# Scaling of v in the first macro step and residuals of the second-layer weights moved to VectorE, with a new table of order numbers

## The chip, the cores and the metric

The kernel runs on one core of a Trainium2 chip. The metric is the device time of one execution in microseconds (us), lower is better. Three runs of the kernel before gave 835.08, 839.51 and 845.69 us, median 839.51 us. PE is TensorE, PEld its weight loads, DVE is VectorE, ACT is ScalarE, POOL is GpSimd, and SP is the engine that issues the DMAs.

## The reference

Three stages follow each other. A delta-rule attention keeps a 48 by 48 state per batch and head (4 batches, 8 heads, 768 steps); a SoLU layer with a layer norm follows (384 to 1024 and back), and then a gated layer (384 to 2048 and back). The inputs are float64.

```python
for t in range(S):
    y[:, :, t] = np.einsum('bhd,bhde->bhe', q[:, :, t], state)
    v_old = np.einsum('bhde,bhd->bhe', state, kt)
    state = state + bt[:, :, :, None] * np.einsum('bhd,bhe->bhde', kt, vt - v_old)
...
h = x @ w_in
sm = e / (np.sum(e, axis=-1, keepdims=True) + 1e-09)
ln = (solu - mu) / np.sqrt(var + 1e-06) * g_ln
...
h = x @ w_in2
g = h * (1.0 / (1.0 + np.exp(-1.702 * h)))
return (g @ w_out2).astype(np.float32)
```

## The kernel before

**Attention.** The 768 steps are cut into 24 blocks of 32 steps, and 4 blocks make a macro step (6 of them). `gram(n)` multiplies the keys of a block with its keys and queries (matmuls of line 568, masked on DVE in lines 583 and 589). `solve(m)` inverts the triangular systems of a macro step on DVE (`halves`, lines 649 to 656, for the first one; the long `eliminate` loop, lines 642 and 645, for the others) and sends the result through DRAM to the tile `dt` (lines 673 and 678). `recur(n)` is the serial part, block after block: v is scaled by a column of `dt` (line 736), the state times the keys is subtracted (748, 752), in the first macro step three products follow (765, 770, 757) with an ACT copy and a DVE subtraction between, the result is copied to `mv` by ACT and DVE (782, 786), the output is multiplied out (792), and the state is updated (827 or 822, then 836).

**Layers.** `layer1(n)` (the A tasks) takes 128 tokens of a block: y is scaled and split into two fp16 halves (`ysb`, lines 856 to 863), transposed by DMA, multiplied with w1 (line 874, 18 matmuls), passes the softmax and the norm on DVE, ACT and POOL (881 to 923) and is transposed by DMA to `lnt`. `layer1_out(g)` (B, line 946, 72 matmuls) takes four blocks together, and `layer2(g)` (C, lines 981 and 1008, 288 matmuls) does the last layer on 512 tokens. Each product is done as three fp16 products of a high and a low half.

**Weights.** `weights()` loads 42 tiles of float64 weights, unpacks each to fp32 on ACT and DVE (lines 479 to 491), writes the high half in fp16 (line 504) and then the residual, the low half. There are two ways for the residual. On PE two products are subtracted in PSUM (line 510, which the trace counts as two matmuls, and line 511) and ACT copies the result out (line 513). On DVE one instruction does it (line 516). The number `pe` says how many tiles, in the order of loading, go the first way: the 6 tiles of w1 and the 8 of wo1 come first, then 12 of w2 (512 columns wide) and 16 of wo2 (384 wide) mixed.

**What sets the order.** All work is given as tasks to `Plan`, with a modelled length, a due time and what it reads and writes. `emit` places one task after another on the engine that could start first, and among tasks that could start together the one with the lowest priority number, the due time plus an entry of the table `OFF` for that task group and engine. So each engine gets one fixed list of instructions, and each engine works through its list in order. Where the plan sees PE with nothing to do, from the start to 7.67 us and again from the end of the first elimination on, it writes filler matmuls of zeros into PE's list (line 351); they keep PE running and give no result. A filler in the list is carried out whether PE would have had to wait there or not.

Of the kernel before, what the change touches and what calls it, by code (L numbers as in the profile page):

```python
# [252 lines left out]
def kernel(  # L253
# [18 lines left out]
    PE, DVE, ACT, POOL, SP = nc.tensor, nc.vector, nc.scalar, nc.gpsimd, nc.sync  # L272
# [26 lines left out]
    w1 = [T("w1h", [128, K0, F1], FP16), T("w1l", [128, K0, F1], FP16)]  # L299
    wo1 = [T("wo1h", [128, K1, DM], FP16), T("wo1l", [128, K1, DM], FP16)]  # L300
# [44 lines left out]
    P = Plan()  # L345
# [7 lines left out]
    U, T0 = PRM["U"], PRM["T0"]  # L353
# [23 lines left out]
    def dve(n, f=1.0):  # L377
        return 0.145 + f * n / 960.0
# [4 lines left out]
    def pool(n):  # L383
        return 0.06 + n * 0.00207
# [296 lines left out]
    def recur(n):  # L681
# [3 lines left out]
        m, s = divmod(n, SUB)  # L685
        base = due(n)
        md = m % 2
        half_ = n >= PRM["nx"] and n < NSUB - 1
        i, ik, iv, ist, ir = n % NKT, n % 2, n % NKV, n % NST, 0
        kr, kt_, v_, st, r_, dt = ktr[i], ktb[ik], vtb[iv], stb[ist], rb[ir], dtb[md]  # L690

        def load_k():
# [3 lines left out]
            if not half_:  # L696
# [3 lines left out]
              nb=base - PRM["ld"])  # L700
# [23 lines left out]
        def load_q():  # L724
            SP.dma_start(out=st[64:64 + D, 0:2], in_=qt[n, 0])
            SP.dma_start(out=st[0:D, 2:4], in_=qt[n, 1])
        P.add("SP", 2 * ISSUE, load_q, w=[f"stq{ist}"], prio=base - 20, lat=0.6, nb=base + 10 - PRM["ld"])

        def load_p():
            for b in range(B):  # L730
                w0 = cls(b)[1]
                SP.dma_start(out=st[w0:w0 + CH, b], in_=p_dr[n % NPD][32 * b:32 * b + 32])
        P.add("SP", 4 * ISSUE, load_p, r=[f"pdr{n % NPD}"], w=[f"stp{ist}"], prio=base - 20, lat=0.35, nb=base + 10 - PRM["ld"])

        dst, dk = (r_, f"r{ir}") if n == 0 else (v_, f"vt{iv}")
        P.add("POOL", pool(384), lambda: POOL.tensor_tensor(
            out=dst, in0=v_, in1=dt[:, s, :, CH:CH + 1].to_broadcast([128, H, D]), op=ALU.mult),
            r=[f"dt{md}_{s}", f"vt{iv}"], w=[dk], prio=base - 5)

        mvs = [f"mvs{c}" for c in range(4)]  # L740
        b1, b2, b3, b4 = Bank(SIDE), Bank(SIDE), Bank(SIDE), [Bank(SIDE), Bank(SIDE)]

        def hd(b):
            return bank(b)[:, 0:H * D].rearrange("p (h c) -> p h c", h=H)

        def ks(h, b):
            r0 = cls(b)[0]
            PE.matmul(hd(b1)[32 * b:32 * b + 32, h, :], lhsT=kr[r0:r0 + D, b % 2, h, :],
# [342 lines left out]
```

## Time and profile before

| what | value |
|---|---|
| median of three runs | 839.51 us |
| the profiled execution: its own time | 836.79 us |
| the profiled execution: its span | 835.1 us |
| PE busy | 777.1 us, 93% of the span |
| DVE busy | 589.5 us, 71% |
| ACT busy | 373.1 us, 45% |
| POOL busy | 247.2 us, 30% |
| mean granted clock of PE | 0.969 |

The span is the time from the first to the last instruction of the profile; the execution's own time is 1.69 us longer. A granted clock of 1.00 is PE at 2.4 GHz, and the lower level is 1.2 GHz, so a mean of 0.85 in a stretch means that PE had the lower level in 30% of it. Starts and ends are in us from the start of the span. Matmuls are pipelined, so the length of a run of equal matmuls is read from start to start.

### The profile page before, as it was taken

What the parts mean: (1) busy time and instruction counts of PE and PEld (TensorE: products, weight loads), DVE (VectorE), ACT (ScalarE), POOL (GpSimd) and SP (SyncE); (2) the same over time, 40 slices, a digit from 0 to 9 for tenths busy, and PEclk for the clock granted to TensorE, in tenths of its full rate; (3) what the DMA queues carried; (4) which work ended last, traced back from release to release, by engine and by line L of the source; (5) the groups of instructions that cost most, each with busy time, mean ns of one, the idle gap of its engine ahead of it and who ended that gap; (6) DMA issues with size and microseconds to landing.
All of it is one profiled execution on the core that took longest, in us unless ns stands there. A gap on an engine that the chain in (4) does not pass through costs nothing.

```text
span 835.1 us, 25208 instructions
## 1 busy us (share of the span) xinstructions
PE 777.1 (93%) x10642; PEld 389.7 (47%) x10642; DVE 589.5 (71%) x1456; ACT 373.1 (45%) x661; POOL 247.2 (30%) x240
## 2 busy tenths in 40 slices
PE   6568978999989999998999999999999999999997
PEld 4135554444555444544544444444444444444443
DVE  2896777999999999999999899964566445212111
ACT  0467564544326524544633545525554355422332
POOL 3020011110413354325531434504442222420322
PEclk7778898999999999999999999999999999999999
DMA  6898597976646466677736654365433252100101
GB/s 168 235 278 232 148 220 137 235 196 168 125 94 139 86 149 171 147 177 159 168 79 187 142 119 104 84 152 144 103 79 94 80 115 44 26 1 0 39 1 38
DMA packets 177314, 105.76 MB, mean 127 GB/s; under 512 B 128273, under 2 KB 161169, under 8 KB 177201
## 3 DMA queue, kind: packets, MB, share of 16 engines
q1 hardware_dynamic: 177200, 104.15, 52.7%
q8 instruction: 83, 1.36, 0.7%
q14 instruction: 31, 0.25, 0.1%
HBM read 66.16 MB, written 20.64 MB: 104 GB/s over the span
## 4 chain that ended last, share of the span: by engine, by line
PE 53%; DVE 27%; issue 9%; DMA 4%; ACT 3%; POOL 2%; POOLq 0%; SPq 0%; ACTq 0%; DVEq 0%
PE psum L1008 13%; PE psum L981 13%; PE psum L946 9%; PE psum L874 6%; DVE mv L836 4%; DVE trip L645 4%; DVE trt L642 4%; PE psum L568 3%; DVE th L989 2%; PE psum L351 2%; DVE mv L786 2%; DVE col L881 2%; PE psum L510 2%; ACT mv L782 2%; DVE eb L893 2%
## 5 line engine op out<-in xcount | busy, mean ns | idle before, releaser
L995 POOL TENSOR_TENSOR gl<-th,gh 128x512 f16<-128x512 f32 x90 | 107.3, 1192 | 236.0 <-ACT gh L992 167.8
L989 DVE SCALAR_TENSOR_TENSOR th<-th,psum 128x512 f32<-128x512 f32 x96 | 65.5, 683 | 89.0 <-ACT th L986 88.4
L1008 PE MATMUL psum<-gl,wo2h 128*128 128x512 f16 x288 | 109.1, 379 | 1.0 <-POOL gl L995 1.0
L1008 PE MATMUL psum<-gh,wo2h 128*128 128x512 f16 x288 | 109.5, 380 | 0.2 <-ACT gh L992 0.2
L981 PE MATMUL psum<-x2th,w2h 128*128 128x512 f16 x288 | 109.5, 380 | 0.1
L981 PE MATMUL psum<-x2th,w2l 128*128 128x512 f16 x288 | 109.1, 379 | 0.0
L981 PE MATMUL psum<-x2tl,w2h 128*128 128x512 f16 x288 | 109.1, 379 | 0.0
L1008 PE MATMUL psum<-gh,wo2l 128*128 128x512 f16 x288 | 109.1, 379 | 0.0
L986 ACT ACTIVATE th<-psum 128x512 f32<-128x512 f32 x96 | 56.9, 593 | 98.4 <-PE psum L981 93.6
L874 PE MATMUL psum<-w1h,xt 128*128 128x512 f16 x288 | 94.2, 382 | 1.5 <-DVE mv L836 0.8
L992 ACT ACTIVATE gh<-th 128x512 f16<-128x512 f32 x96 | 60.2, 627 | 68.9 <-DVE th L989 64.6
L1008 PEld LDWEIGHTS <-wo2h 128*128 128x128 f16 x576 | 56.2, 98 | 67.9 <-issue 2.1
L981 PEld LDWEIGHTS <-w2h 128*128 128x128 f16 x576 | 53.5, 98 | 62.0 <-issue 0.3
L642 DVE TENSOR_TENSOR trt<-trip 128x30 f32<-128x30 f32 (+9 forms) x150 | 71.3, 476 | 2.7
L645 DVE TENSOR_TENSOR trip<-trip,trt 128x30 f32<-128x30 f32 (+9 forms) x150 | 69.6, 464 | 2.4
L923 POOL TENSOR_TENSOR lnr<-eb,lnr 128x1024 f16<-128x1024 f32 x24 | 52.2, 2173 | 52.0 <-ACT lnr L921 52.0
L874 PEld LDWEIGHTS <-xt 128*128 128x128 f16 x432 | 40.0, 98 | 49.9 <-issue 2.5
L890 ACT ACTIVATE eb<-psum,col 128x512 f32<-128x512 f32 x48 | 36.9, 773 | 52.4 <-DVE col L886 52.1
L946 PE MATMUL psum<-lnth,wo1h 128*128 128x512 f16 x144 | 54.6, 379 | 0.4 <-DVE th L989 0.4
L874 PE MATMUL psum<-w1l,xt 128*128 128x512 f16 x144 | 54.8, 381 | 0.0
L946 PE MATMUL psum<-lnth,wo1l 128*128 128x512 f16 x144 | 54.6, 379 | 0.0
L946 PE MATMUL psum<-lntl,wo1h 128*128 128x512 f16 x144 | 54.6, 379 | 0.0
(210 smaller groups left out, 1246.6 us busy)
## 6 DMA issues: line engine op xcount, KB each, us to landing
kq<-kq SPq DMA_DIRECT2D x44, 192.0 KB, 4.4
stg<-w_in SPq DMA_DIRECT2D x11, 512.0 KB, 5.6
vt<-vt SPq DMA_DIRECT2D x24, 192.0 KB, 2.7
st<-qt SPq DMA_DIRECT2D x48, 96.0 KB, 2.9
kt<-kdr SPq DMA_DIRECT2D x48, 96.0 KB, 2.3
stg<-udr SPq DMA_DIRECT2D x48, 96.0 KB, 2.3
out<-ob SPq DMA_DIRECT2D x18, 256.0 KB, 2.7
ktr<-kd SPq DMA_DIRECT2D x46, 96.0 KB, 2.9
```

Source lines behind the costliest of these rows:

```text
L642: DVE.tensor_tensor(out=tv, in0=tri[:, lo:hi, j:j + 1].to_broadcast([128, nr, j]), in1=tri[:, j:j + 1, 0:j].to_broadcast([128, nr, j]), op ...
L645: DVE.tensor_tensor(out=tri[:, lo:hi, 0:j], in0=tri[:, lo:hi, 0:j], in1=tv, op=ALU.add)
L874: PE.matmul(bank(bh[j]), lhsT=x[:, k], rhs=w_[:, k, 512 * j:512 * j + 512], start=(k == 0 and i == 0), stop=(k == K0 - 1 and i == 2))
L890: P.add("ACT", act(512) + 0.34, lambda j=j, ev=ev: ACT.activation(out=ev, in_=bank(bh[j]), func=ACTF.Exp, bias=cl(3), scale=cl(0), accum_o ...
L923: P.add("POOL", pool(F1), lambda: POOL.tensor_tensor(out=lnr[1], in0=e_, in1=lnr[0], op=ALU.subtract), r=["lnrh"] + [f"eb{ie}_{j}" for j i ...
L946: PE.matmul(bank(ba)[:, 0:w_], lhsT=wo1[a][:, k, oc], rhs=lnt[b][:, k, tk], start=(k == 0 and i == 0), stop=(k == K1 - 1 and i == 2))
L981: PE.matmul(bank(bh)[:, 0:w_], lhsT=w2[a][:, k, fc], rhs=x2t[b][:, k, tk], start=(k == 0 and j == 0), stop=(k == K0 - 1 and j == 2))
L986: P.add("ACT", act(w_), lambda: ACT.activation(out=th, in_=bank(bh)[:, 0:w_], func=ACTF.Tanh, scale=0.851 / (X2S * W2S)), r=[bh], w=[f"th{ ...
L989: P.add("DVE", dve(w_), lambda: DVE.scalar_tensor_tensor(out=th, in0=th, scalar=1.0, in1=bank(bh)[:, 0:w_], op0=ALU.add, op1=ALU.mult), r= ...
L992: P.add("ACT", act(w_), lambda: ACT.activation(out=gh, in_=th, func=ACTF.Copy), r=[f"th{i}"], w=[f"gh{i}"], prio=base)
L995: P.add("POOL", pool(w_), lambda: POOL.tensor_tensor(out=gl, in0=th, in1=gh, op=ALU.subtract), r=[f"th{i}", f"gh{i}"], w=[f"gl{i}"], prio= ...
L1008: PE.matmul(bank(acc[o])[:, 0:w_], lhsT=wo2[a][:, f, oc], rhs=gb[i][b][:, 0:w_], start=(f == 0 and j == 0), stop=(f == K2 - 1 and j == 2))
```

## The change

Three things are changed. The scaling of v for blocks 0 to 3 (`m == 0`) goes from POOL to DVE. `pe` goes from 38.322 to 14, so that only the tiles of w1 and wo1 get their residual on PE, and the 24 tiles of w2 and wo2 that did so before get it on DVE, where the last four already were. And all numbers of `OFF` are new, so every engine has another order.

```diff
-OFF = {'gram0|SP': 42.93, 'gram0|PE': 207.21, 'gram0|DVE': 422.4,
+OFF = {'gram0|SP': -73.65, 'gram0|PE': 157.32, 'gram0|DVE': -184.67,
...
-PRM = dict(bl=161.965, vm=-0.684, vo=-1.262, pe=38.322, near=22.976,
+PRM = dict(bl=161.965, vm=-0.684, vo=-1.262, pe=14, near=22.976,
...
         dst, dk = (r_, f"r{ir}") if n == 0 else (v_, f"vt{iv}")
-        P.add("POOL", pool(384), lambda: POOL.tensor_tensor(
+        eng, cost, E_ = ("DVE", dve(384), DVE) if m == 0 else ("POOL", pool(384), POOL)
+        P.add(eng, cost, lambda: E_.tensor_tensor(
             out=dst, in0=v_, in1=dt[:, s, :, CH:CH + 1].to_broadcast([128, H, D]), op=ALU.mult),
-            r=[f"dt{md}_{s}", f"vt{iv}"], w=[dk], prio=base - 5)
+            r=[f"dt{md}_{s}", f"vt{iv}"], w=[dk], prio=base - 5, port=True)
```

The diff puts one more line into the kernel, so line 736 and all behind it have a number higher by one in the changed kernel.

**PE, from the last matmul of block 3's first layer to the first of B0.** Before, this piece of the list holds the last w1 product of block 3 (`xt_95`), four gram quads (line 568), fillers (`zeros_157`) and four residual tiles (`eye`, `neg`). Before:

```order
L874 MATMUL psum_69<-w1h,xt_95 128x512
L568 MATMUL psum_70<-kq_112 32x64 x32
L351 MATMUL psum_63<-zeros_157 128x512
L510 MATMUL psum_66<-fst_89,eye 128x512
L511 MATMUL psum_66<-w2h,neg 128x512
L510 MATMUL psum_70<-fst_89,eye 128x384
L510 MATMUL psum_66<-ob_109,eye 128x384
L510 MATMUL psum_68<-ob_110,eye 128x512
L946 LDWEIGHTS wo1h
```

Now:

```order
L875 MATMUL psum_70<-w1h,xt_95 128x512
L351 MATMUL psum_63<-zeros_157 128x512
L568 MATMUL psum_67<-kq_112 32x64 x32
L568 MATMUL psum_69<-kq_111 32x64 x32
L568 MATMUL psum_70<-kq_112 32x64 x32
L947 LDWEIGHTS wo1h
```

Rows that repeat are left out. The residual tiles are gone from the piece, the four gram quads stay, and the fillers go from 55 to 126 (15, 10, 47, 11 and 43 between the quads). In the whole list the fillers go from 128 to 245 and the residual tiles from 38 to 14.

**DVE, the norm of block 3** (`col_138` holds its column of numbers; lines 901 and 908 are the end of the first and the start of the second part of the norm, between which ACT squares the row). Before:

```order
L901 TENSOR_TENSOR col_138<-col_138 128x1
L645 TENSOR_TENSOR trip<-trip,trt 128x28x3
L583 TENSOR_TENSOR gsb_122<-psum_70,mask 128x256
L642 TENSOR_TENSOR trt<-trip 128x108
L583 TENSOR_TENSOR psb_124<-psum_70,mask 128x256
L645 TENSOR_TENSOR trip<-trip,trt 128x27x4
L481 TENSOR_SCALAR stg_86<-stg_86 128x384
L642 TENSOR_TENSOR trt<-trip 128x130
L908 SCALAR_TENSOR_TENSOR col_138<-col_138 128x1
```

Now, the first rows behind the end of the first part, two of the three residuals that stand there, and the last rows:

```order
L902 TENSOR_TENSOR col_138<-col_138 128x1
L645 TENSOR_TENSOR trip<-trip,trt 128x28x3
L481 TENSOR_SCALAR wo2l<-wo2l 128x384
L642 TENSOR_TENSOR trt<-trip 128x108
L483 SCALAR_TENSOR_TENSOR fst_87<-fst_87,wo2l 128x384
L516 SCALAR_TENSOR_TENSOR wo2l<-fst_87,wo2h 128x384
L516 SCALAR_TENSOR_TENSOR w2l<-fst_89,w2h 128x512
L645 TENSOR_TENSOR trip<-trip,trt 128x22x9
L642 TENSOR_TENSOR trt<-trip 128x210
L909 SCALAR_TENSOR_TENSOR col_138<-col_138 128x1
```

Between the two parts stood 7 instructions and stand 27 now. From the `ysb` instruction of block 3 (line 863) to the last column instruction of its norm (line 916) there were 65 and are 91.

**DVE, the first scalings of v.** The scaling (line 737) of blocks 0 and 1 now stands among the unpacking of weights:

```order
L491 SCALAR_TENSOR_TENSOR fst_88<-stg_86,fst_88 128x512
L481 TENSOR_SCALAR wo2l<-wo2l 128x384
L483 SCALAR_TENSOR_TENSOR w2l<-w2l,wo2l 128x384
L737 TENSOR_TENSOR rb_132<-vt_120,dt_130 128x384
L491 SCALAR_TENSOR_TENSOR w2l<-wo2l,w2l 128x384
L737 TENSOR_TENSOR vt_121<-vt_121,dt_130 128x384
L516 SCALAR_TENSOR_TENSOR w2l<-fst_88,w2h 128x512
```

Before, these were the first work that POOL had after its constants, with nothing of its list in front; now 20 DVE rows stand between the end of the solve's output and the first of them.

## Rows read from the trace of the kernel before

**Rows 1.** The page: span, and busy time (share of the span) of each engine.
```profile
span 835.1 us, 25208 instructions
PE 777.1 (93%) x10642; PEld 389.7 (47%) x10642; DVE 589.5 (71%) x1456; ACT 373.1 (45%) x661; POOL 247.2 (30%) x240
```
**Rows 2.** Busy time by stretch: stretch, its length, engines (instructions), clock, DMA share.
```profile
core 0: us, PE busy (x) PEld busy (x) DVE busy (x) ACT busy (x) POOL busy (x), PEclk, DMA share, GB/s
0.00:46.00 46.00, 24.06 (x552) 12.22 (x552) 25.86 (x78) 13.08 (x22) 7.57 (x30) 0.74 0.76 219
46.00:138.50 92.50, 77.75 (x1756) 46.19 (x1756) 68.86 (x165) 56.17 (x112) 12.11 (x8) 0.85 0.83 196
138.50:175.94 37.44, 36.19 (x623) 19.52 (x624) 34.26 (x106) 18.58 (x32) 5.52 (x4) 1.00 1.00 207
175.94:700.00 524.06, 509.94 (x7117) 253.53 (x7116) 434.42 (x1062) 239.15 (x420) 184.97 (x167) 1.00 0.55 128
700.00:835.10 135.10, 129.17 (x597) 58.22 (x595) 26.10 (x48) 46.11 (x76) 37.05 (x31) 1.00 0.09 21
```
**Rows 3.** Waits of PE from 46 to 176 us: line, waited for, us, times, longest.
```profile
PE psum L748 <- issue: 4.8, 2, 2.5
PE psum L792 <- DVE mv L786: 2.3, 1, 2.3
PE psum L827 <- issue: 1.9, 1, 1.9
PE psum L765 <- issue: 1.4, 1, 1.4
PE psum L568 <- issue: 0.8, 1, 0.8
```
**Rows 4.** Timeline of PE at three places of the recurrence: start, us, what.
```profile
138.50 0.89 PE L792 MATMUL psum<-mv,st 112*32 112x48 f32 x64 [2.29 <-DVE mv L786]
...
150.69 0.39 PE L874 MATMUL psum<-w1h,xt 128*128 128x512 f16 x1 [0.43 <-DMA xt<-ysb]
...
175.94 0.38 PE L946 MATMUL psum<-lnth,wo1h 128*128 128x512 f16 x1
```
**Rows 5.** Timeline of PE: gram quad, fillers, residual tiles; read start to start.
```profile
157.97 1.10 PE L568 MATMUL psum<-kq 48*32 48x64 f32 x64
159.00 2.98 PE L351 MATMUL psum<-zeros 128*128 128x512 f16 x13
161.82 1.02 PE L510 MATMUL psum<-fst,eye 128*128 128x512 f32 x2
...
162.89 1.67 PE L351 MATMUL psum<-zeros 128*128 128x512 f16 x7
...
172.61 0.81 PE L510 MATMUL psum<-fst,eye 128*128 128x384 f32 x2
...
173.42 0.81 PE L510 MATMUL psum<-ob,eye 128*128 128x384 f32 x2
```
**Rows 6.** Timelines of POOL and PE at the first scaling of v.
```profile
58.22 3.35 POOL L736 TENSOR_TENSOR rb<-vt,dt 128x384 f32<-128x384 f32 x1 [49.19 <-DMA dt<-ddr]
...
61.62 0.57 PE L765 MATMUL psum<-rb,dt 32*32 32x48 f32 x34 [2.18 <-POOL rb L736]
```
**Rows 7.** Instructions of the v scaling: count, shortest/median/longest ns, first and last start.
```profile
L736 POOL TENSOR_TENSOR vt<-vt,dt x23: 837/843/1286, 61.5 to 661.8; 128x384 f32<-128x384 f32 x23
```
**Rows 8.** Instructions of the residual on DVE, columns as in the group before.
```profile
L516 DVE SCALAR_TENSOR_TENSOR wo2l<-ob,wo2h x2: 549/550/550, 195.6 to 203.1; 128x384 f16<-128x384 f32 x2
```
**Rows 9.** Timeline of DVE in the norm of block 3, and POOL beside it.
```profile
142.61 0.62 DVE L863 SCALAR_TENSOR_TENSOR ysb<-psum,col,ysb 128x384 f16<-128x384 f32 x1
...
164.01 0.16 DVE L916 TENSOR_TENSOR col<-col 128x1 f32<-128x1 f32 x1
...
169.67 2.29 DVE L642 TENSOR_TENSOR trt<-trip 128x198 f32<-128x198 f32 x1
...
169.45 2.29 POOL L923 TENSOR_TENSOR lnr<-eb,lnr 128x1024 f16<-128x1024 f32 x1 [5.67 <-ACT lnr L921]
```

More of the change, by code (lines that the diff above doesn't have):

```diff
@@ new lines @@
+PRM = dict(bl=161.965, vm=-0.684, vo=-1.262, pe=14, near=22.976, al=0.0, af=0.658, xp=25.764, lp=1.945, go1=24.87, so1=49.904, ew=48, nx=6.743, kp=13.711, need=100.793, fg=0.161, f1=7.669, f3=1796.849, sp=0.084, gp=0.667, gq=99, cold=25.151, cf=-1.14, nb4=9.499, v1b=1.424, cut=0.473, el=22.0, la=0.602, d0=-55.31, d1=-18.518, d2=6.18, d3=1.2, a0=14.438, wo1s=1.606, nk=15.164, nb2=1.269, nb3=7.307, early=21.447, v1=-9.577, wa=0.829, U=36.161, T0=31.882, g0=0.697, a=-0.318, b=0.937, ao=18.661, go=231.282, gs=-2.989, so=-0.04, ss=0.661, w1=-840.745, wo1=-7.28, w2o=-52.255, w2s=8.446, wo2o=41.493, wo2s=4.056, nb=1.319, bs=0.333, cs=4.152, su=8.832, ld=47.69)
```

3 lines of the change are left out of this document (1 added, 2 removed).

## The prediction

> **What bounds the kernel now.** I read the page first: PE is busy for 93% of the span, the next engine for 71% [rows 1]. So a change can pay in two ways only: less work on PE, or less waiting of PE. Next I read the busy times by stretch [rows 2]. From 175.94 us, where the first product of B0 starts [rows 4], to the end PE is busy 509.94 + 129.17 = 639.1 of 659.2 us, at the full clock; that part is PE's own work. Before it PE is idle for 21.9 + 14.8 + 1.3 = 38.0 us, and from 46 to 138.5 us it runs at a mean clock of 0.85, which is the lower level in 30% of the time. The change acts almost only in this first part. Third, the waits of PE there [rows 3]: the four kinds called "issue", in which PE waits for nothing that the profile shows, sum to 8.9 us, and the longest wait for an engine within the recurrence is 2.3 us, for DVE. Fourth, the timeline [rows 4]: the fourth output product of the recurrence starts at 138.50, block 3's first layer at 150.69, B0 at 175.94. I use the first and the last of these as cuts, so the span has three pieces: up to 138.50, the 37.44 us to B0, and the 659.2 us after.
>
> **The prices.** From [rows 5], start to start at the full clock: 13 fillers from 159.00 to 161.82 are 0.217 each; a residual tile of 512 columns from 161.82 to 162.89 is 1.07; one of 384 columns from 172.61 to 173.42 is 0.81; a gram quad from 157.97 to 159.00 is 1.03. Two matmuls of a first layer stand for 0.43, as two fillers do, since they have the same shape.
>
> **The residuals leave PE, and fillers come in.** The 24 tiles are 12 of 512 and 12 of 384 columns: 12 x 1.07 + 12 x 0.81 = 22.6 us less on PE. The list has 117 fillers more: 117 x 0.217 = 25.4 us. So PE as a whole gets 2.8 us more to do, and the question is only where. I count the lists by the three pieces.
> - Up to 138.50, from the first product of the recurrence at 61.62 [rows 6]: 14 tiles fewer (7 of each width, -13.2), 47 fillers more (+10.2), one gram quad fewer (-1.0), three first-layer matmuls more (+0.6): -3.3 us at the full clock. At the clock of this stretch that is 3.3 / 0.85 = 4.0. Its bounds are 0 (PE would have waited there for the recurrence anyway) and 6.6 (all of it at the lower level). I take 4.0, since the mean clock is the nearest row.
> - From there to B0: 7 tiles fewer (3 of 512, 4 of 384, -6.4), 92 fillers more (+20.0), a quad more (+1.0), three first-layer matmuls fewer (-0.6): +13.9 us. PE is idle for 37.44 - 36.19 = 1.25 us of this stretch [rows 2] and at the full clock, so work that is put into its list can hide 1.25 us at most: +12.7 to +13.9. I take 12.7. This is the firmest term of the sum, because fillers are in PE's list whatever happens elsewhere, and the B0 products stand behind them.
> - After B0: two tiles of 512 fewer (-2.1), one quad fewer (-1.0), two fillers fewer (-0.4): -3.6 us, PE's own work, so it counts in full. Bounds: the 20.1 us in which PE is idle after B0 can shrink or grow with the new order; I take half of it each way as its bound, 10 us, and zero as the value.
>
> ACT loses 24 copies out of PSUM. It is idle for 36 of 92.5 us in the second stretch [rows 2], and the long waits of the recurrence are not for it [rows 3], so a freer ACT is worth nothing here; it could only bring copies to `mv` forward, and then the state update on DVE is what comes late next.
>
> **The residuals on DVE.** One takes 0.55 us at 384 columns [rows 8], of 512 columns none is in the trace: between the 0.55 and, in proportion to the columns, 0.73; I take 0.7. 24 are about 15 us on DVE, and 20 of all residuals stand ahead of B0's first result now. DVE is busy for 34.26 of the 37.44 us ahead of B0 [rows 2], so here it could become late. Its list from block 3's `ysb` to the end of that block's norm has 91 instructions in place of 65; the 65 took 142.61 to 164.17, 21.6 us or 0.33 each [rows 9], so 26 more are 8.6 us. The way from `ysb` to B0 took 175.94 - 142.61 = 33.3 and would take 41.9; counted from the cut, 4.1 us earlier, that is 46.0 us. PE's list needs 37.44 + 12.7 = 50.1 us for the same way. So the residuals on DVE are hidden behind the fillers, with 4.1 us to spare. Where they aren't, every us beyond these 4.1 counts.
>
> The Trainium skill, page "Perfetto Trace Analysis", section "Optimizing Scalar/DVE Operations", speaks against this part: where the Vector engine is saturated, it would give work away to Scalar or even GPSIMD, and this change does the reverse. By it the 8.6 us would count in full instead of nothing; by the rows of the lists they lie behind fillers, and I keep the sum and give the rule a rival.
>
> **The scaling of v.** The first one took 3.35 us on POOL [rows 6], four times the 0.84 us of the others [rows 7], and PE's first product waited for it. On DVE it is one operation on 384 columns, like the residual: 0.55. The gain is 2.8 us if DVE takes it up at once. The 20 rows ahead of it are mostly unpacking work that DVE had at that time before as well; if six of them are still ahead when `dt` lands, at 0.55 each, the gain turns into 6 x 0.55 - 2.8 = 0.5 of loss. These are the bounds; I take 2.8, since DVE has the same work there as before. The other three scalings were done long before they were needed: nothing, and 1.7 us more on DVE behind PE's work.
>
> **The sum.** -2.8 (v) - 4.0 (recurrence) + 12.7 (fillers ahead of B0) - 3.6 (after B0) = +2.3 us. The profiled execution took 836.79 us, so 839.1; the median of the runs was 839.51, 2.7 us above that execution and well inside the spread of the runs. I predict 839 us.
>
> **The rivals.**
> - *The recurrence becomes quick.* For it: its stretch from 61.62 to 138.50 holds 8.9 us of "issue" waits [rows 3] and half-clock running worth 0.15 x 65 = 9.8 us (65 being 84% of the 76.9 us, the busy share of the second stretch in [rows 2]). With residuals gone from between its products, both could vanish: 839 - 8.9 - 9.8 = 820 us. Against it: fillers stand at the same places, nothing in the change takes away an "issue" wait, and PE's list does not get shorter. 15%.
> - *DVE becomes late* (the skill's rule). Place: the first macro step. 12 residuals (6.5 us at about 0.55) and four scalings (2.2 us) stand in DVE's list ahead of block 3's `ysb`, and the products of the recurrence wait for DVE at each block. If they all lie on the path, the gains of 2.8 and 4.0 are lost and 8.7 us come on top; and if POOL and DVE hold each other up as at 169.45, where an elimination step took the 2.29 us of the POOL operation beside it [rows 9], twice in the norm of block 3, that is 4.6 and uses up the 4.1 that were spare. Then 839 + 6.8 + 8.7 = 855, and 859 with two more such holds. It decides from the point at which DVE's queue adds more than 6.8 us to the recurrence. 12%.
> - *The change does nothing*, since fillers took the place of the tiles and the spare time is used elsewhere: 836 to 838 us. It can't be told from my forecast by the time, only by the place of B0, and is part of it.
>
> The forecast has 73%; its own range is 828 to 850 (the distances of the bounds from the values taken, 10 us for the waits after B0 among them, as the root of the sum of their squares: 10.3 down, 11.3 up). With part of the two rivals, the range for 8 times in 10 is 821 to 855. About 2% is what a measurement of this kernel can tell from no change, here 16.8 us: faster means under 822.7, slower over 856.3. The first rival ends at the edge of that, the second mostly inside it: 0.14 faster, 0.76 same, 0.10 slower.
>
> **What would show it.** In the profile after, the first recurrence product should start about 2.8 us after `dt` lands sooner than before, the fourth output product near 132, and B0 near 181 with PE at the full clock and without idle time for about 50 us before it; from B0 to the last instruction there should be about 655 us. The forecast is wrong if B0 starts before 170 or after 190, or if PE waits for DVE for more than 5 us between the two cuts.

## The result, and the profile after

The changed kernel takes 845.01 us (median of 20 runs, 840.08 to 850.09) against 839.52 us for the kernel before (20 runs, 832.69 to 850.84): a ratio of 1.0074, with a 95% interval of 1.0051 to 1.0098. It is 0.7% slower. No change was forecast, at 839.0 us. The time lies inside the range, but the whole interval of the ratio lies above 1, and two of the four terms of the sum missed by 5 and 9 us, in opposite directions.

The page of the changed kernel, span and engines, answers to [rows 1]:

```profile
span 838.4 us, 25263 instructions
PE 775.9 (93%) x10687; PEld 386.5 (46%) x10687; DVE 584.9 (70%) x1484; ACT 363.0 (43%) x637; POOL 244.6 (29%) x236
```

PE is busy for 1.2 us less than before here, and for 5.4 us more in the second profiles below (773.7 and 779.1 us); the prediction had counted 2.8 us more. DVE has 28 instructions more and is yet busy for 4.6 us less; the last section comes back to that. The same kernel by stretch, columns as in [rows 2], cut at its own B0:

```profile
0.00:46.00 46.00, 25.19 (x555) 12.68 (x556) 27.95 (x82) 13.43 (x22) 7.56 (x30) 0.73 0.79 220
46.00:138.50 92.50, 80.84 (x2106) 47.11 (x2105) 79.35 (x203) 48.86 (x95) 6.05 (x4) 0.95 0.86 207
138.50:172.37 33.87, 33.32 (x389) 16.42 (x388) 30.03 (x92) 13.65 (x22) 8.08 (x4) 1.00 1.05 216
172.37:700.00 527.63, 504.55 (x6980) 250.47 (x6981) 419.03 (x1056) 239.24 (x421) 185.88 (x167) 1.00 0.55 126
700.00:838.40 138.40, 132.03 (x670) 59.84 (x668) 28.58 (x56) 47.80 (x78) 37.07 (x31) 0.99 0.08 21
```

Behind B0, PE is busy for 504.55 + 132.03 = 636.6 of 666.0 us: 29.4 us idle, where it was 20.0 before. Its timeline at the places of [rows 4] and [rows 6] (first product of the recurrence, fourth output product, block 3's first layer, the fillers ahead of B0, B0):

```profile
56.54 0.36 PE L766 MATMUL psum<-rb,dt 32*32 32x48 f32 x14 [0.53 <-DVE rb L737]
...
121.11 0.27 PE L793 MATMUL psum<-mv,st 112*32 112x48 f32 x2
...
135.84 0.39 PE L875 MATMUL psum<-w1h,xt 128*128 128x512 f16 x1 [1.17 <-DMA xt<-ysb]
...
163.08 9.45 PE L351 MATMUL psum<-zeros 128*128 128x512 f16 x43
172.37 0.38 PE L947 MATMUL psum<-lnth,wo1h 128*128 128x512 f16 x1
```

One profile is one execution, and this one took 840.1 us, the shortest of its 20 runs. So both kernels were profiled a second time.

**Two more profiles.** No edit.

> The kernel before, profiled a second time: how far the pieces of one profile can be trusted. If they repeat, first product at 61 to 62 us, B0 at 175 to 177, tail 658 to 661 with 19 to 21 us of PE idle. If one execution is only a draw, the tail is 663 us or more, and the 659.2 that the prediction's sum used was a short one.

> The changed kernel, profiled a second time, since the profile shown (840.1 us) is the shortest of its runs (median 845.0). If pieces repeat, first product at 56 to 58 us, B0 at 172 to 173, tail 665 to 667 us. If the first profile was a lucky draw in the first macro step: first product at 59 to 61, B0 at 175 to 177; if in the tail: a stretch of lower clock there, tail 669 us or more.

Measured: 837.35 and 845.11 us. The two last stretches (B0 to 700 us, 700 us to the end) of the kernel before, second profile:

```profile
173.12:700.00 526.88, 509.46 (x7115) 253.08 (x7114) 437.49 (x1057) 238.94 (x419) 184.82 (x167) 1.00 0.54 127
700.00:835.60 135.60, 129.74 (x600) 58.46 (x598) 26.59 (x51) 46.35 (x76) 37.06 (x31) 1.00 0.09 21
```

and of the changed kernel, second profile:

```profile
176.50:700.00 523.50, 499.32 (x6890) 248.05 (x6889) 417.29 (x1041) 235.87 (x414) 185.79 (x166) 1.00 0.54 126
700.00:843.40 143.40, 136.98 (x752) 62.24 (x750) 32.51 (x69) 50.96 (x86) 37.61 (x32) 0.99 0.08 21
```

By the same cuts, from the two profiles of each (us):

| piece | before | changed | difference of means | forecast |
|---|---|---|---|---|
| to the first product | 61.6, 62.4 | 56.5, 58.1 | -4.7 | -2.8 |
| to the fourth output product | 76.9, 73.9 | 64.6, 67.8 | -9.2 | -4.0 |
| to B0 | 37.4, 36.9 | 51.3, 50.6 | +13.8 | +12.7 |
| B0 to the end | 659.2, 662.5 | 666.0, 666.9 | +5.6 | -3.6 |
| PE busy behind B0 | 639.1, 639.2 | 636.6, 636.3 | -2.7 | -3.6 |
| PE idle behind B0 | 20.0, 23.3 | 29.4, 30.6 | +8.3 | 0 (10 either way) |

The first three pieces sum to -0.1 us: B0 starts at 175.9 and 173.1 us before, at 172.4 and 176.5 after. The whole difference, 5.5 us, stands behind B0, and is the difference of the medians. Both expectations of a lucky draw came true in part: the 659.2 us on which the sum rested was a short one, and the changed kernel's first macro step was 4 us quicker in the first profile than in the second.

The waits of PE from B0 to the end show where the 8.3 us lie (line, waited for, us, times, longest). Before, first profile:

```profile
PE psum L792 <- ACT mv L782: 3.5, 6, 1.1
PE psum L748 <- DVE mv L836: 3.3, 11, 0.6
PE psum L792 <- DVE mv L786: 2.0, 6, 0.7
PE psum L757 <- DVE rb L752: 1.9, 3, 1.4
PE psum L1008 <- POOL gl L995: 1.0, 2, 0.7
PE psum L874 <- DVE mv L836: 0.8, 2, 0.6
```

After, first profile (lines one higher):

```profile
PE psum L793 <- ACT mv L783: 3.5, 10, 0.8
PE psum L793 <- DVE mv L787: 3.3, 8, 1.1
PE psum L758 <- DVE rb L753: 3.0, 6, 0.8
PE psum L1009 <- POOL gl L996: 2.6, 5, 0.7
PE psum L749 <- DVE mv L837: 2.5, 8, 0.6
PE psum L875 <- DMA xt<-ysb: 2.0, 2, 1.3
PE psum L793 <- DVE fst L802: 1.7, 1, 1.7
```

No wait is longer than 1.7 us, and no engine stands out: the loss is many waits under 1 us, at products of the recurrence (L793, L758), at the second layer's products for `gl`, at first layers for their transposed input. And DVE does not have more to do there: from B0 to 700 us it is busy for 434.4 and 437.5 us before, for 419.0 and 417.3 after. PE and DVE both idle more. That reads as an order of work that fits less well; the experiments ask whether it is that.

### The profile page after: what moved, and what is told of

It reads as the page before. It is cut to its first block, busy times and chain, and to the rows that moved or that the text cites. A ratio compares the mean times of both kernels' runs of the same rounds, so it can differ in the third digit from the quotient of the medians.

```text
span 838.4 us, 25263 instructions
## 1 busy us (share of the span) xinstructions
PE 775.9 (93%) x10687; PEld 386.5 (46%) x10687; DVE 584.9 (70%) x1484; ACT 363.0 (43%) x637; POOL 244.6 (29%) x236
## 5 line engine op out<-in xcount | busy, mean ns | idle before, releaser
L982 PEld LDWEIGHTS <-w2h 128*128 128x128 f16 x576 | 54.3, 98 | 64.6 <-issue 1.3
L924 POOL TENSOR_TENSOR lnr<-eb,lnr 128x1024 f16<-128x1024 f32 x24 | 54.7, 2281 | 53.7 <-ACT lnr L922 53.6
L645 DVE TENSOR_TENSOR trip<-trip,trt 128x30 f32<-128x30 f32 (+9 forms) x150 | 67.3, 449 | 2.3
L912 POOL TENSOR_TENSOR col<-col,half 128x1 f32<-128x1 f32 x24 | 14.5, 604 | 180.7 <-DVE col L910 143.5
L351 PE MATMUL psum<-zeros 128*128 128x512 f16 x245 | 60.0, 393 | 7.4 <-DVE zeros L350 6.8
L642 DVE TENSOR_TENSOR trt<-trip 128x30 f32<-128x30 f32 (+9 forms) x150 | 63.6, 424 | 2.2
L891 ACT ACTIVATE eb<-psum,col 128x512 f32<-128x512 f32 x48 | 36.9, 773 | 58.3 <-DVE col L887 58.2
L837 DVE SCALAR_TENSOR_TENSOR mv<-psum,mv 48x384 f32<-48x384 f32 x92 | 51.1, 555 | 5.8 <-PE psum L823 3.6
```

The lines of the kernel that those rows point to most:

```text
L351: P.fill.append((gate, until, lambda: PE.matmul(psum[0], lhsT=z, rhs=z.unsqueeze(1).to_broadcast([128, 4, 128]), start=True, stop=True)))
L642: DVE.tensor_tensor(out=tv, in0=tri[:, lo:hi, j:j + 1].to_broadcast([128, nr, j]), in1=tri[:, j:j + 1, 0:j].to_broadcast([128, nr, j]), op ...
L645: DVE.tensor_tensor(out=tri[:, lo:hi, 0:j], in0=tri[:, lo:hi, 0:j], in1=tv, op=ALU.add)
L924: P.add("POOL", pool(F1), lambda: POOL.tensor_tensor(out=lnr[1], in0=e_, in1=lnr[0], op=ALU.subtract), r=["lnrh"] + [f"eb{ie}_{j}" for j i ...
L982: PE.matmul(bank(bh)[:, 0:w_], lhsT=w2[a][:, k, fc], rhs=x2t[b][:, k, tk], start=(k == 0 and j == 0), stop=(k == K0 - 1 and j == 2))
```

## The experiments

**How an order was held.** The planner makes another order whenever a task changes its engine, so a part of the change cannot be undone in the source without all tasks moving. So most kernels here take their order, filler counts and PSUM banks from a table; with a kernel's own table this gives that kernel's own instruction lists.

```
-    def emit(self, sem=SEM, log=None):
-        ...                                  # choose the next task by priority and modelled time
+    def emit(self, log=None):
+        for item in ORDER.split():           # task, fillers ahead of it, banks
+            at, n, banks = re.match(r"(\d+)(?:f(\d+))?((?:b\d)*)$", item).groups()
+            ...
+            for _ in range(int(n or 0)):
+                self.fill[0][2]()
+            t.fn()
```

**1. The changed kernel, behind B0 in the old order.**

```
 ORDER = changed kernel's up to the first product of B0
-        + changed kernel's from there
+        + what is left, in the order of the kernel before
```

> The changed code in the changed order up to the first product of B0; from there on the tasks stand in the order that the kernel before has. Theory A (the loss lies in the order after B0, which puts less other work between dependent products): B0 starts near 172.4 us as in the changed kernel, the rest takes 657 to 660 us instead of 666.0, so the span is about 831 and the ratio to the kernel before 0.992 to 0.996. Rival B (the first macro step leaves its work behind: what DVE or the queues have not done at B0 is paid for later): the rest stays at 665 to 667 us, ratio 1.006 to 1.008. In between, both have a part.

Measured: ratio 1.0109 (1.0063 to 1.0155); B0 at 177.4, the rest 669.5 us, PE idle for 29.8. Theory A fails here: the old order is no better behind the new first macro step. The clock shows one reason. This kernel from 184 us on, columns as in [rows 2]:

```profile
184.00:196.00 12.00, 10.88 (x110) 5.20 (x109) 9.61 (x22) 4.64 (x9) 0.00 (x0) 1.00 0.44 144
196.00:202.00 6.00, 1.55 (x7) 0.55 (x6) 5.75 (x18) 2.64 (x5) 0.00 (x0) 0.90 0.28 89
202.00:208.00 6.00, 6.00 (x75) 2.73 (x73) 5.90 (x17) 2.02 (x4) 0.00 (x0) 0.53 0.38 87
```

PE waited for 4.45 of 6 us, and then ran the next 6 us at nearly the lower level. With a second such place at 244 to 256 us this cost some 5 us ((1 - 0.90) x 6 + (1 - 0.53) x 6, and 1.7 by the same sum at the second). From the second block of 512 tokens on (first product of B1) the old order takes 539.0 us here, and 535.1 and 538.4 in the two profiles of its own kernel (541.5 with v on DVE, experiment 5); so most of what it lost, it lost in the first block, at the seam, where one order goes over into the other (130.6 us to B1 instead of 124.1 in both profiles before).

**2. The kernel before, behind B0 in the new order.**

```
 ORDER = kernel before's up to the first product of B0
-        + kernel before's from there
+        + what is left, in the order of the changed kernel
```

> The code before in the order before up to the first product of B0; from there on the order of the changed kernel. Theory A: B0 near 175.9 us, the rest 666 to 669 us (two residual tiles of PE remain, 2.1 us), ratio 1.008 to 1.012. Rival B: the rest stays at 659 to 661, ratio 0.999 to 1.002.

Measured: 1.0114 (1.0068 to 1.0160); B0 at 177.9, the rest 672.0 us, PE idle for 29.6 us. As theory A had it, with a longer rest. Here too the clock fell twice (220 to 232 and 244 to 256 us, some 3.5 us); without that and the 2.1 us of two tiles it is 666.4, the time of the changed kernel. From B1 on the new order takes 542.4 us here, 541.9 and 542.2 in its own kernel. The idle time of the whole rest tells little, since it was 29.8 us in experiment 1 too, in the old order. From B1 on, where no seam disturbs, PE is idle for 21.8 us here, for 21.8 and 22.3 in the changed kernel, and in the old order for 14.9 and 18.4 (the two profiles before), 18.7 (1) and 21.1 (5). The old order takes 535.1 to 541.5 us there (these four executions, mean 538.5), the new one 541.9 to 542.4 (three). The experiments still to come narrow this: 3, 6, 7 and 8, in the old order, take 539.6, 541.3, 540.9 and 541.3 us from B1 on, and 4, in the new one, 541.5, so that the means are 2.4 us apart (539.6 and 542.0) and the ranges touch.

What the order does by itself shows best at the output products of the recurrence. Behind B0 they wait 5.3 to 6.5 us in all in eight executions of the old order (both profiles before, 1, 3, 5, 6, 7, 8), whatever the code, and 8.5 to 9.4 us in four of the new one (both profiles of the changed kernel, 4, and this one with the old code). Step by step the waits are those of the order: at steps 9, 16 and 17 they are 1.44, 1.12 and 1.03 us here, 1.09, 1.65 and 1.03 in the first profile of the changed kernel, and 0.23, 0 and 0 in the first before.

**3. The new code in the old order, nothing in place of the tiles.**

```
 ORDER = kernel before's, task by task
-PE, ACT   residual of w2/wo2 tile, copy     x24
+DVE       residual of w2/wo2 tile           x24
-POOL      scaling of v, n = 0 to 3
+DVE       scaling of v, n = 0 to 3
```

> The changed code (24 residuals and the four scalings of v on DVE) with every task at the place that it has in the kernel before, and with that kernel's 128 fillers, so that no filler takes the place of the tiles. Theory A (DVE has room for the residuals; only fillers and the new order ate the gain): PE has 20 us less to do ahead of B0, of which about half shows, since chains through DVE end there: B0 near 165, the rest 656 us, ratio 0.985 to 0.990. Rival C (DVE becomes late): 15 us more on DVE lie on the way, B0 at 180 to 188, ratio 1.004 to 1.013.

Measured: 1.0066 (1.0037 to 1.0096); B0 at 174.7, the rest 668.2. Neither place of B0 was right: PE had 22.6 us less to do, and B0 came when it always comes. Its stretch from 46 to 138.5 us shows what went against it:

```profile
46.00:138.50 92.50, 71.74 (x1710) 44.96 (x1710) 76.66 (x185) 49.73 (x98) 5.71 (x4) 0.75 0.83 204
```

The mean clock is 0.75, where it was 0.85 and 0.92 in the two profiles before and 0.95 and 0.91 in those of the changed kernel. Experiment 8, the same kernel with 98 fillers in place of the tiles, has 0.91. So the residual tiles had kept PE busy between the small products of the recurrence, and without them or fillers the lower clock takes back what their absence gives: the recurrence to its fourth output product takes 80.1 us, not less than the 76.9 and 73.9 before.

**4. The changed kernel with 54 fillers fewer ahead of B0.**

```
 PE, ahead of the gram quad at 162 us:
-    11 fillers
 PE, ahead of the first product of B0:
-    43 fillers
```

> The changed kernel without the last two groups of fillers ahead of B0 (43 and 11, 54 x 0.217 = 11.7 us of PE). Theory of the prediction (the way through DVE from block 3's output to B0 has 4.1 us to spare behind the fillers): B0 4.1 us earlier, near 168.3, PE idle for about 7.6 us where the fillers stood, ratio 1.002 to 1.004. Rival D (only the fillers hold B0): B0 near 160.7, ratio 0.993 to 0.995. Rival E (the granted clock falls to its lower level in the gap): a mean clock under 1.0 in the 20 us around B0 and B0 not earlier than 172 us, ratio 1.006 or more. The part after B0 is the same in all three, 664 to 667 us.

Measured: 1.0073 (1.0040 to 1.0106), the changed kernel's time. From the fourth output product to B0 it takes 49.4 us, 1.6 us less than the mean of the two executions with all fillers, though 11.7 us of fillers are gone. PE's timeline ahead of B0:

```profile
156.73 6.21 PE L255 MATMUL psum<-zeros 128*128 128x512 f16 x28
162.87 1.99 PE L472 MATMUL psum<-kq 48*32 48x64 f32 x128
172.69 0.59 PE L851 MATMUL psum<-lnth,wo1h 128*128 128x512 f16 x1 [7.83 <-DMA lnth<-lnr]
```

Where the fillers stood, PE waits 7.83 us for the transposes of block 3's norm. So B0 is held by the way through that norm, which DVE has in its list between other work, and the fillers cover this way; they don't make it longer. The end of the first part of the norm and the start of the second stand in DVE's timeline, first profile before and then first profile of the changed kernel, at:

```profile
160.85 0.16 DVE L901 TENSOR_TENSOR col<-col 128x1 f32<-128x1 f32 x1
...
162.75 0.22 DVE L908 SCALAR_TENSOR_TENSOR col<-col 128x1 f32<-128x1 f32 x1
```

```profile
147.94 0.16 DVE L902 TENSOR_TENSOR col<-col 128x1 f32<-128x1 f32 x1
...
160.82 0.22 DVE L909 SCALAR_TENSOR_TENSOR col<-col 128x1 f32<-128x1 f32 x1
```

Between the two parts lie 1.9 us before and 12.9 us in the changed kernel (1.9 and 12.6 in the second profiles, 12.4 here). In experiments 3, 6 and 8, which have the residuals on DVE but the old order, it is 2.3 us. So the place that the norm got in DVE's new list, and not the residuals by themselves, uses up what the quicker recurrence had gained. The forecast had 4.1 us to spare behind the fillers; it is 1.6. Rival D falls. Rival E's numbers came, though not as its reason had it: B0 is late for the transposes, and the clock falls in the gap and is down behind it (mean 0.50 from 172 to 178 us, 0.74 to 184), which is about 4 us of the 670.2 us that the rest takes, and the time is no shorter. So these 54 fillers neither cost nor gain: what their absence gives at B0 the clock takes back.

**5. The scaling of v alone, old order.**

```
-        P.add("POOL", pool(384), lambda: POOL.tensor_tensor(
+        eng, cost, E_ = ("DVE", dve(384), DVE) if m == 0 else ("POOL", pool(384), POOL)
+        P.add(eng, cost, lambda: E_.tensor_tensor(
```

> The kernel before in its own order, with the four scalings of v on DVE in place of POOL and nothing else. Theory of the prediction: the first product comes 2.3 to 2.8 us earlier (near 59) and the whole kernel with it, ratio 0.996 to 0.998, the tail after B0 at 659 to 662 us. Rival (something else holds the recurrence or B0, the DMA of the weights for one): the first product earlier, but B0 within 1 us of 175.9 and ratio 0.999 to 1.001. That would also mean that the 2.8 us of the sum were never to be had.

Measured: 0.9992 (0.9965 to 1.0019). The first product starts at 58.6 us, 3.4 earlier than the mean before, so the local gain is there; B0 starts at 175.5. The rival holds: the gain ends in the recurrence, whose fourth output product is at 138.5, as in [rows 4] (136.3 in the second profile before).

**6. The residuals alone, old order, fillers at the tiles' places.**

```
-PE, ACT   residual of w2/wo2 tile, copy     x24
+DVE       residual of w2/wo2 tile           x24
+PE        5 (512 columns) or 4 (384) fillers, at the 22 places ahead of B0
```

> The kernel before in its own order, v on POOL, with the 24 residuals on DVE; at the places of the 22 tiles that stood ahead of B0 PE gets fillers of the same length (5 for 512 columns, 4 for 384; 98 in all), so that it has the same work and the same claim to its clock as before. Theory A (what the change loses is lost by PE's order, not by DVE): B0 at 175 to 178 us, mean clock of 46 to 138.5 us at 0.83 to 0.87, tail 656 to 661 us with 19 to 22 us of PE idle, ratio 0.997 to 1.002. Rival C (DVE, busy over 90% of the time from 46 to 500 us, gets late by the residuals): B0 at 180 or later or the tail at 664 to 670 with 26 us of idle or more, ratio 1.006 to 1.015. Where the clock lies under 0.83, the fillers did not replace the tiles and the run says nothing of DVE.

Measured: 1.0030 (1.0006 to 1.0054); clock 0.89 from 46 to 138.5 us, so PE kept it; B0 at 174.8, the rest 667.3, PE idle for 29.2. Now the order is the same, DVE has the 24 residuals more (0.54 to 0.69 us each, one of 1.17), and it is slower, by less than rival C had it. One place can be read. DVE, which has no idle time here, and then PE:

```profile
195.10 0.68 DVE L420 SCALAR_TENSOR_TENSOR w2l<-fst,w2h 128x512 f16<-128x512 f32 x1
...
200.17 1.90 DVE L567 TENSOR_TENSOR dsb<-trip,nrm 128x1024 f32<-128x1024 f32 x1
202.00 0.67 DVE L893 SCALAR_TENSOR_TENSOR th<-th,psum 128x512 f32<-128x512 f32 x1
```

```profile
202.72 0.38 PE L885 MATMUL psum<-x2th,w2h 128*128 128x512 f16 x1 [3.49 <-DVE th L893]
```

PE's next group waits 3.49 us for DVE's `th`, which stands in DVE's list behind the residual and the 1.90 us of the solve. Before, with B0 1.2 us later, DVE did this `th` at 200.71, 1.29 us sooner.

**7. The same, the two late residuals left on PE.**

```
-        if nst[0] <= PRM["pe"]:
+        if nst[0] <= PRM["pe"] or (name, c0) == ("w2", 1536) and k > 0:
```

> The kernel with fillers for the 22 tiles (the old order, v on POOL, ratio 1.003), but the two residuals that stand behind B0 stay on PE as in the kernel before; 22 are on DVE. Theory H (behind B0 DVE has no idle time and PE waits for it product by product, so that the late residuals count there): the waits of 1.2 and 3.5 us at 195 and 203 us and the lower clock behind them go, tail 661 to 664 us in place of 667.3, ratio 0.997 to 1.001. Rival I (the 22 early residuals cost the 0.3%, through DVE's backlog at B0): tail 665 to 668, ratio 1.002 to 1.005.

Measured: 1.0038 (1.0008 to 1.0069), the rest 665.3 us. The 3.49 us wait falls to 1.06, and PE's idle time in the first block from 7.7 to 5.1 us, as theory H had it, but the time does not follow: rival I by the ratio. How the 22 early residuals cost time behind B0, which starts no later than before (175.6 us), these profiles don't show.

**8. Both parts of the code, old order, fillers at the tiles' places.**

```
 the table of 6, and
-POOL      scaling of v, n = 0 to 3
+DVE       scaling of v, n = 0 to 3
```

> Both parts of the change (24 residuals and the four scalings of v on DVE), every task at its place in the kernel before, and 98 fillers at the places of the 22 tiles that stood ahead of B0, so that PE's claim to its clock stays. Against the changed kernel (ratio 1.0074) only the order differs. Theory J (the new order costs as much as the code): 0.3% for the residuals less 0.1% for v, ratio 1.001 to 1.004, tail 663 to 667 us. Rival K (the code costs all of it, and the parts add up badly when DVE gets both): ratio 1.006 to 1.009, tail 667 us or more. A ratio of 1.005 tells neither.

Measured: 1.0036 (1.0009 to 1.0062), the rest 666.7 us. Theory J. The code change, with its fillers, costs about 0.36% in the old order; the changed kernel costs 0.74%, which leaves 0.38% to the new order. From the half widths of the two intervals that difference is uncertain by 0.36% (the root of 0.24 squared plus 0.27 squared), so that the order has a part is just shown, the halves are not. The changed kernel differs from this one by its 19 further fillers too (245 to 226). And the profiles don't show where its part lies: the rest takes 666.7 us here, at the border between the two theories, and 666.0 and 666.9 in the changed kernel, and B0 is at 172.6 against 172.4 and 176.5.

**9. More cover in the changed kernel.** Between the small products of a step (`dr`, whose result ACT and DVE copy, and `ym`, which needs the copies) the lists have groups of three large matmuls, 0.65 us each. Behind B0 the old order has three or more such groups between them at every step; the new one has two at steps 5, 8 and 22, two with a gram quad at 7, 12 and 15, and one with a gram quad at 6 and 14.

```
 PE, step 9:
-  dr9  C1 C0 C0        ym9  C1 C1
+  dr9  C1 C0 C0 C1 C1  ym9
 PE, step 12:
-  C1 C1     dr12  gram21 C1 C1  ym12  C1 C1
+  C1 C1 gram21 C1 dr12 C1 C1 C1 ym12
 ... (11 output products by 1 to 3 groups, 4 products ahead of them by 1)
```

> The changed kernel, with the order of PE alone altered behind B0: at 11 steps of the recurrence the output product stands one to three groups of three large matmuls (0.65 us each) further behind the product whose copies it waits for, at 4 steps the product ahead of it one group. Nothing else moves. Theory F (the loss after B0 is a lack of cover: where two groups stand between dependent products in place of three, PE waits): of the 12 to 13 us that these products wait after B0 in the two profiles of the changed kernel, 8.9 go (6.7 at output products, 2.2 at the others); PE idle after B0 from 30 to about 21, tail 657 to 659 us, ratio 0.996 to 0.999. Rival G (the recurrence or DVE is the bound; a product that stands later only passes its wait on to the next one): idle stays at 27 to 31, tail 664 to 668, ratio 1.005 to 1.009.

Measured: 1.0139 (1.0095 to 1.0183); the rest 673.1 us, PE idle for 35.0. The waits that were to go did go: the output products wait 2.1 us behind B0 instead of 8.7 and 9.4, the products ahead of them 0.5 instead of 3.0 and 3.7. And others came. This kernel's longest from B0 on (L913 and L886 are the second layer's products, L779 the first layer's):

```profile
PE psum L913 <- POOL gl L900: 5.2, 8, 1.1
PE psum L886 <- DVE fst L706: 4.1, 2, 2.2
PE psum L779 <- DVE eb L798: 3.4, 1, 3.4
PE psum L779 <- DMA xt<-ysb: 2.1, 3, 1.4
```

The groups that now stand ahead of `ym` wait themselves, because DVE does its list in its own order. At one of them DVE's timeline reads:

```profile
339.60 0.55 DVE L691 COPY mv<-psum 32x384 f32<-32x384 f32 x1
341.19 0.56 DVE L691 COPY mv<-psum 32x384 f32<-32x384 f32 x1 [1.04 <-ACT mv L687]
341.78 0.56 DVE L706 SCALAR_TENSOR_TENSOR fst<-psum,dt 128x384 f32<-128x384 f32 x1
```

while PE's next group, `psum<-x2th,w2h`, waits 2.23 us to 342.40 for a bank. Rival G, and worse than it had it. Some 5 us of the rest are the clock's: behind PE's wait of 3.4 us for `eb` at 243 us it is 0.50 from 244 to 250 us. Altering the order of one engine alone did not mend this kernel. Nor is the count of groups the whole of it: at the eight steps named above, where the new order has fewer than three whole groups, the output products wait 4.0 us in all in the new order and 3.3 in the old (means of the four and the eight executions of experiment 2), at the steps with three or more 5.0 and 2.8. So most of the longer waits stand where the cover was not short by this count.

**10. The same in the kernel before, with v on DVE.**

```
 PE, step 14:
-  dr14  C2 C2 C2        ym14  C2 C2
+  dr14  C2 C2 C2 C2 C2  ym14
 ... (10 output products by 1 or 2 groups, 2 products ahead of them by 1)
```

> The kernel before in its own order, v on DVE, residuals on PE as before, with the same treatment: 10 output products one or two groups later, two products ahead of them one group. Theory F: 5.9 us of waits go (5.4 and 0.5), PE idle after B0 from 20 to 26 (three executions of this order) to 15 to 20, tail 655 to 660 us, ratio 0.990 to 0.994; it would beat both kernels. Rival G: tail as in those executions, 659 to 666 us, ratio 0.997 to 1.001.

Measured: 0.9968 (0.9936 to 1.0000), the rest 662.6 us, PE idle for 23.0. The ratio lies just under rival G's range and above theory F's, and the idle time is the mean of the three earlier executions of this order (23.1). The output products wait 0.6 us instead of 5.5 and 6.5, and it comes back elsewhere (`gl` 3.4 us instead of 1.0). It has the lowest ratio of the study, below the changed kernel's 1.0074; against the kernel before its interval just reaches no change, and from v alone (0.9992, experiment 5) it can't be told apart.

**11. Less cover in the kernel before.**

```
 PE, step 14:
-  dr14  C2 C2 C2  ym14  C2
+  dr14  C2 C2  ym14  C2 C2
 ... (the output products of steps 6 to 23, one group earlier)
```

> The kernel before, untouched but for the output products of steps 6 to 23 of the recurrence, which stand one group of three large matmuls earlier: the cover is taken away that the changed order lacks. Theory F: ten of these steps wait already and would wait 0.65 us longer, 6.5 us; the other eight between nothing and 5.2 us; PE idle after B0 26 to 34 us, tail 667 to 674, ratio 1.007 to 1.014. Rival G: no change beyond 2 us, ratio 0.998 to 1.002.

Measured: 1.0098 (1.0064 to 1.0131), the rest 672.7 us, PE idle for 28.5. Its longest waits from B0 on:

```profile
PE psum L696 <- ACT mv L686: 7.4, 10, 1.6
PE psum L696 <- DVE mv L690: 5.6, 15, 1.4
PE psum L652 <- DVE mv L740: 2.8, 9, 0.6
```

The output products (L696) wait 13.0 us instead of 5.5 and 6.5, 6.5 to 7.5 more, as theory F had it. PE is busy for 644.2 us instead of 639.1 and 639.2 as well, and the clock fell twice (0.76 from 472 to 478 us, 0.75 from 496 to 502). So a group of cover taken away costs time at once; a group added, against the order of the other engines (9 and 10), gives back a little or nothing.

## Why the prediction was wrong

- **The failed step is the third item of the fillers and tiles, "After B0".** It was put at -3.6 us, "PE's own work, so it counts in full", with zero for the change of PE's waits there. PE's work fell by 2.7 us, near the forecast; its waits grew by 8.3, inside the bound of 10 that was set and then valued at zero. Zero was a choice without a row behind it. The old order was known to leave 20.1 us of waits there; of a new order nothing in the trace could say that it would leave no more, and the lists, which could be read, showed a sign of it: two groups where three had stood. That sign alone points at the smaller part of the longer waits (9). The time came within 6 us of the forecast partly by luck: the three pieces up to B0 were to add 5.9 us and added nothing, while the piece behind B0 was to save 3.6 and cost 5.6.
- **What caused it.** The code, put into the old order with fillers, costs 0.36%, the new order about as much again (8). That the order has a part of its own shows in 2, where it brings its waits at the output products to the code before, some 3 us of the 8.3. How the early residuals cost time behind B0, and what else of the 8.3 us the order makes, stays open. Theory A as first put, that all of it is the order, fell with 1 and 6.
- **v: -2.8 forecast, -3.4 where done alone (5), -4.7 in the two profiles of the changed kernel.** Right at its place, and nearer than -4.7 says: experiments 1, 4 and 9 have the changed kernel's lists up to there and start the first product at 59.8, 60.8 and 61.1 us, 2 and 11 have the old ones and start it at 61.5 and 61.9, and over all of these the difference is -2.6. (The count of fillers left out the list ahead of that product, which has 20 fewer, 28 for 48. It cost nothing, since PE waits for the scaled v there all the same, 2.18 us before and 0.53 after.) It was worth 0.7 us of 840 in the end (0.9992, within its interval of nothing), because the recurrence behind it did not end earlier.
- **The recurrence: -4.0 forecast, -9.2 measured.** The first rival (15%) was half right. PE's idle time in this piece fell from 11.9 and 12.5 us to 8.2 and 7.4; the "issue" waits from 46 to 172 us from 8.9 in both profiles to 4.3 and 6.4. Nine fillers stood in it before, 56 now, between the products; what was held against that rival, that fillers stand at the same places, was wrong. With the same further executions the piece differs by -10.2 us, of which PE's idle time makes some 3.4 and the shorter list, as counted, 3.3. The mean clock of the piece is 0.85 to 0.93 in the four executions of the old lists and 0.90 to 0.97 in the five of the new; the rest would be its part, and is uncertain. The "issue" waits vary as well: 7.7 and 7.4 us in 1 and 9, with the changed kernel's lists, and 3.4 to 4.5 in 6 to 8, with the old order. Fillers at the tiles' own places keep the clock, but gain nothing here: the piece takes 74.3, 76.7 and 77.7 us in 6 to 8, 80.1 without them (3).
- **To B0: +12.7 forecast, +13.8 measured, and the reason was half wrong.** The fillers are in PE's list, but 11.7 us of them taken out brought 1.6 us (4). From the fourth output product through block 3's norm to B0 it took 49.4 us there, not 46.0. From block 3's `ysb` to the end of its norm DVE takes 34.6 and 32.2 us in the changed kernel and 21.6 and 21.2 before, 12.0 more where the forecast, at 0.33 us for each of 26 instructions, had 8.6. That the output comes earlier and B0 does not is the same thing: B0 starts at 172 to 178.5 us in every kernel here, whatever PE has to do ahead of it.
- **DVE becomes late (12%).** Not at the place named: B0 is not late, since block 3's `ysb` comes 10.6 us earlier and its norm takes 12.0 us longer. But residuals, in the old order, on DVE with PE's list made up by fillers cost 0.30, 0.38 and 0.36% (6 to 8). The Trainium skill, page "Perfetto Trace Analysis", section "Optimizing Scalar/DVE Operations", finds that it may make sense to offload some work from a saturated Vector engine. This change does the reverse, and the three runs agree with the page in sign, with 2.5 to 3.2 us where the rule, as the forecast read it, would have had 8.6. A residual of 512 columns takes 0.67 to 0.70 us, but for one of 0.87 in each profile of the changed kernel; 0.7 was assumed.
- **The base.** The 659.2 us behind B0 came from one execution; the same list took 662.5 and, with v on DVE, 665.5 in others. A term of 3.6 us was smaller than the spread of the piece that it was taken from. The 2% that the forecast held for the least that can be told from no change was too coarse: 20 runs of each kernel told 0.74%, to within 0.24.

## What to carry to other kernels

When a change makes a planner redraw the whole order, the terms of the edit are the small part: forecast a loss behind the edit too, and don't value a bound of 10 us at zero. Counting in the new lists how much independent work stands between dependent products gives the sign, but here found the smaller part of the longer waits. Look also at how far apart the parts of one chain come to stand on another engine's list: block 3's norm lost 11 us in that way, about as much as the recurrence ahead of it gained. Work taken off PE in a stretch of small products gained nothing where it was what kept the clock up (3); ask what will keep it busy instead. Profile twice before a term of a few us is read as a difference of two pieces.

## What was not expected of the hardware

- **More instructions on DVE in the same time.** With 28 instructions more, DVE's busy time is 589.5 and 593.7 us before, 584.9 and 588.6 after. The elimination steps of the solve became shorter, and an operation of the norm took half its time. DVE by line, second profile before (count, busy us, mean ns, idle before):

```profile
L645 DVE TENSOR_TENSOR trip<-trip,trt 128x30 f32<-128x30 f32 (+9 forms) x150 | 74.7, 498 | 2.4
L642 DVE TENSOR_TENSOR trt<-trip 128x30 f32<-128x30 f32 (+9 forms) x150 | 70.2, 468 | 2.7
L915 DVE SCALAR_TENSOR_TENSOR col<-col 128x1 f32<-128x1 f32 x24 | 9.3, 386 | 2.0 <-POOL col L911 1.8
```

and second profile after:

```profile
L645 DVE TENSOR_TENSOR trip<-trip,trt 128x30 f32<-128x30 f32 (+9 forms) x150 | 69.1, 461 | 2.3
L642 DVE TENSOR_TENSOR trt<-trip 128x30 f32<-128x30 f32 (+9 forms) x150 | 63.4, 423 | 2.2
L916 DVE SCALAR_TENSOR_TENSOR col<-col 128x1 f32<-128x1 f32 x24 | 4.4, 184 | 1.9 <-POOL col L912 1.8
```

  In the second profiles, of the 300 elimination steps, the 207 that run with no POOL instruction beside them take 327 ns before and (208) 323 after; the 93 and 92 beside POOL take 830 and 710. It is not their size: a step of line 642 on 30 elements takes 190 ns without and 962 ns with POOL beside it (five each, second profile before). The operation of the norm takes about 0.15 us by itself in the first profiles; six of its 24 stood beside a POOL operation before and took 1.0 to 1.1 us, three did after and took 0.2 to 0.85. So the time of DVE's work depends on what POOL does beside it: in the new order as many steps meet POOL, but each loses less, and that is part of what makes up for the 24 residuals.
- **A wait of a few us behind B0 costs again.** In experiments 1, 4 and 6, PE idle for 3.5 to 7.8 us was followed by a slice of 6 us at a mean clock of 0.53, 0.50 and 0.72. A long wait is not the only thing that goes ahead of it: in experiment 2 the clock fell to 0.77 from 220 to 226 us, among small products, with no wait of PE over 0.5 us from 208 to 226. The two kernels themselves show the upper level in every slice from B0 until PE's work runs out, in all four profiles.
- **The spread is made in few places.** With one list, B0 (175.9, 173.1) and the second block (B1 to B2: 125.7 and 128.7 us in the kernel before) differ between executions by 3 us, while many waits at a given product repeat to 0.01 us (the output products of steps 5, 8, 9, 11, 14, 17 and 22 in the changed kernel: 0.32, 0.32, 1.09, 0.70, 0.56, 1.03 and 0.32 us in both profiles).
